# The expert stage of an attention and mixture-of-experts kernel: its engines put in one written order, weight splits placed between the products and their halves

## The chip, the cores and the metric

One core of one Trainium2 chip runs the kernel as a single launch. The metric is the device time of one execution in microseconds (us). The engines are TensorE (PE in the profile, with its weight loads apart as PEld), VectorE (DVE), ScalarE (ACT), GpSimd (POOL) and SyncE (SP, whose queue issues most of the transfers).

## What is computed

Three stages follow each other: causal attention with a bias, a mixture of 8 experts of which each token uses one, and a dense two-layer network on the experts' outputs.

```python
attn = softmax(q @ k.T / 8 + min(bias, 0), causal) @ v      # 4 x 8 heads, 576 tokens, 64 wide
x = attn as 2304 rows of 512
e = argmax(x @ w_gate); gate = softmax(x @ w_gate)[e]
x = gate * (relu(x @ w1[e]) @ w2[e])                        # w1 512 x 1024, w2 1024 x 512, per expert
h = x @ w_in; out = (h * clip(h + 3, 0, 6) / 6) @ w_out     # 512 x 2048, 2048 x 512
```

All of it is wanted in float32 quality. The kernel splits each float32 number into a 16-bit high half and a 16-bit rest, and each product of two matrices becomes three matmuls (high by high, high by rest, rest by high).

## The kernel before

The change is in the expert stage. It runs 10 **passes** over sorted tokens: two of 224 rows for experts 0 and 1 (passes 0 and 1), then one for each expert, the fullest first, of 336, 336, 336, 312, 296, 280, 136 and 104 rows (passes 2 to 9). A pass has an **f half**, eight first products `ph` (`expert_hidden`, L1002, 12 matmuls each), and a **d half**, four second products `py` (L1090, 24 matmuls each).

- After a first product ACT writes the high half of `hT` (`Relu`, L1006) and DVE the rest (L1007). A second product reads all eight of them, `hT` 0 first. After a second product DVE multiplies by the tokens' gates (`y`, L1096, from the transfer `held`, L1056), ACT writes the high half into `x2T` (L1097) and POOL the rest (L1098). ACT also fills the part of `x2T` that a pass may leave over with zeros (L1069, four times in a pass).
- The weights of pass p + 1 are loaded and split during pass p. They are eight **pieces** of 512 KB (`wf`, L228, on SP's queue), four of `w1` and four of `w2`, into five buffers. In passes 2 to 7 two further pieces hold the dense network's `w_in` (`wd`, L967), which arrives as **doubles**: ACT takes the absolute value (L972), POOL bounds it (L974), DVE shifts and joins (L975, L979, L980), ACT writes the high half (L981), DVE the rest (L982).
- `piece(..., act)` says who splits. False: POOL writes the high half (L239), DVE the rest (L240). True: ACT writes the high half (L237). 2: ACT writes the high half (L232), POOL scales in place (L233) and writes the rest (L234), and DVE has no part.
- The tokens of pass p + 1 come by a chain of transfers: `slots` (the list of rows, L200, SP), a gather `xg` of 128 rows at a time (L207, POOL), and a transpose of each gathered tile into `xsT` (L211, SP).
- `feed(k)`, called after each product, issues up to k loads and lets the oldest of them be split while more than four are outstanding. A split is one call: all the instructions of the piece.

In the attention stage the order on each engine is fixed by `in_order`. In the expert stage it is not: a scheduler arranges the instructions of each engine by its own estimate, held only by dependencies and by a few `issue_after` marks. Each engine then runs its list strictly from the front, so an instruction that waits holds up all behind it.

Pass 0 also takes in the last attention units' router work: three small products (`pl`, L608), `route`, `place_tokens` (which writes each token's row to `tok_d` by five scatters, L677) and `counts`, by the list `hooks`. `slots` of pass 2 and later can only be read behind those scatters.

Of the kernel before, what the change touches and what calls it, by code (L numbers as in the profile page):

```python
# [33 lines left out]
def kernel(  # L34
# [225 lines left out]
    def w2_jobs(src, ring="even", act=False):  # L260
# [6 lines left out]
                lambda f: f.rearrange("p (a n) -> p a n", a=2), act,  # L267
# [4 lines left out]
    with ExitStack() as at:  # L272
# [584 lines left out]
        for us in groups:  # L857
# [9 lines left out]
            for g, u in sorted(enumerate(us), key=lambda x: place[x[1]]):  # L867
# [7 lines left out]
                if us[0] == min(late) and place[u] >= NU - 3:  # L875
                    hooks.setdefault(min(len(hooks), 4), []).append(lambda u=u, mms=mms: mms[u]())
                    continue
                at_time(t + d, lambda u=u, mms=mms: mms[u]())
                routed = max(routed, t + d + 1.0)
            if us[0] == min(late):  # L880
                hooks.setdefault(4, []).append(lambda us=us: list(route(us)))
                hooks.setdefault(4, []).append(lambda us=us: (list(place_tokens(us)), counts()))
# [15 lines left out]
        w0 = w1_jobs(of(0), act=2)  # L898
        splits = {}

        def w_load(x):
            if x == len(w0):
                w0.extend(w2_jobs(of(0), act=2))
# [56 lines left out]
    def double_piece(src, hi, lo):  # L960
# [4 lines left out]
        def ld():  # L965
# [3 lines left out]
            def sp():  # L969
# [4 lines left out]
                gts(out=mf, in0=mf, scalar1=3.0e38, scalar2=2.0**-15, op0=ALU.min, op1=ALU.max)  # L974
                nc.vector.tensor_scalar(  # L975
# [20 lines left out]
    def expert_hidden(wt, xT, n, hT, f):  # L996
# [3 lines left out]
        for c in range(KD):  # L1000
            for x, (a, b_) in enumerate(((0, 0), (0, 1), (1, 0))):
# [3 lines left out]
                ).ins  # L1005
        mark["act"] = nc.scalar.activation(hT[0][:, f, :n], ph[:, :n], AF.Relu).ins  # L1006
# [13 lines left out]
    with ExitStack() as ex_:  # L1020
# [5 lines left out]
        xsT = xs0[0]  # L1026
        for p, rows in enumerate(passes):
            jobs = []
            nxt = None
            if p + 1 < NPASS:  # L1030
                nxt = load_x(p + 1)
                ring = "even" if p % 2 else "odd"
                jobs = w1_jobs(of(p + 1), ring, p == 0) + w2_jobs(of(p + 1), ring, p == 0)
                if 2 <= p <= 7:
                    jobs += djobs[:2]
                    del djobs[:2]
            hT = [e2.tile([128, KF, CAP], F16, tag=f"hT{x}", name="hT") for x in range(2)]
            wt1, wt2 = wts[p % 2], wts[2, p % 2]
            pend, fed = [], [0]

            def feed(k):
                for ld in jobs[:k]:
                    with tc.issue_after(mark["x" if fed[0] < KD or ("xs", 1) not in mark else ("xs", 1)]):
                        pend.append(ld())
                    fed[0] += 1
                del jobs[:k]
                while len(pend) > (8 if hooks else 4 if jobs else 0):
                    with tc.issue_after(mark["pos"]):
                        pend.pop(0)()

            for f in range(KF):
                expert_hidden(wt1, xsT, rows, hT, f)
                if f == 4:
# [7 lines left out]
                if p == 0:  # L1061
                    for h in hooks.pop(f, []):
                        h()
                if p and f % 2 == 1:

                    a, z = (min(sum(passes[:x]), NT) for x in (p, p + 1))
                    if z > a:
                        with after("act"):
                            nc.scalar.activation(  # L1069
                                x2T[:, f // 2::KD, a:z], zero16[:, None].to_broadcast([128, 2, z - a]), AF.Copy  # L1070
                            )
                feed(1 + f % 2)
            if NS <= p + 2 < NPASS:
                load_slots(p + 2)
# [10 lines left out]
            for d in range(KD):  # L1085
# [8 lines left out]
                hi, lo = x2T[:, d, at_], x2T[:, KD + d, at_]  # L1094
# [5 lines left out]
            xsT = nxt  # L1100
# [181 lines left out]
```

## Time and profile before

| | |
|---|---|
| median of 3 runs | 968.99 us (967.59 to 971.37) |
| the profiled execution's own time | 966.54 us |
| its span, first to last instruction | 964.8 us |
| mean granted TensorE clock | 0.932 of full speed |
| busy in the span: PE, DVE, ACT, POOL | 87%, 56%, 36%, 43% |
| expert stage, first `ph` to the first product of the dense network | 264.1 to 561.7 us |

Times in views are from the span's start. The span is 1.7 us shorter than the execution. Busy time of PE counts matmuls at whatever clock was granted, so a slow clock looks like work.

### The profile page before, as it was taken

Reading aid. Unit: us, or ns where it says so; the run is one execution under the profiler, and the core shown is the slowest. Engines: PE = TensorE matmul, PEld = TensorE weight load, DVE = VectorE, ACT = ScalarE, POOL = GpSimd, SP = SyncE. Lnnn points to the kernel's source line nnn. Section 1 sums busy time; section 2 is a strip of 40 time slices with the busy share of each in tenths; the row PEclk is TensorE's granted clock in tenths of the full one; section 3 lists DMA queues with packets and bytes.
Section 4 is the critical chain, followed back from the end, with each engine's and each line's share of the span. In section 5 each row is a group of like instructions: output and inputs, shape, how many; then the busy total and the mean of one; then the engine's idle time right before and its main releaser. Section 6 shows DMA issues by size and latency. Waiting matters only on the chain. (4 is left out here: it accounts for less than half of the span.)

```text
span 964.8 us, 17003 instructions
## 1 busy us (share of the span) xinstructions
PE 843.3 (87%) x6402; PEld 516.6 (54%) x6402; DVE 545.1 (56%) x1206; ACT 345.7 (36%) x684; POOL 410.6 (43%) x451
## 2 busy tenths in 40 slices
PE   7899998888785968888887799987999999999993
PEld 5566666655574735556665654433444444447441
DVE  5668877768544658967677649997044025105000
ACT  5687677665532303223222234433022012002000
POOL 2863564954735747745734624442022012112010
PEclk9899999779787979889989899997999999999997
DMA  9788649324577997797879513321000000000000
GB/s 244 164 163 214 112 100 266 67 78 89 96 183 171 205 230 236 212 263 178 265 158 204 160 43 108 124 88 45 34 12 0 22 22 1 12 22 12 22 23 24
DMA packets 140746, 112.71 MB, mean 117 GB/s; under 512 B 114760, under 2 KB 115024, under 8 KB 140144
## 3 DMA queue, kind: packets, MB, share of 16 engines
q1 hardware_dynamic: 136816, 101.43, 44.5%
q0 software_dynamic: 3840, 10.12, 3.2%
q8 instruction: 52, 0.85, 0.4%
q14 instruction: 38, 0.31, 0.1%
HBM read 91.82 MB, written 9.62 MB: 105 GB/s over the span
## 5 line engine op out<-in xcount | busy, mean ns | idle before, releaser
L1014 PE MATMUL py<-wo,gT 128*128 128x512 f16 x864 | 190.8, 383 | 5.7 <-ACT wo L981 3.8
L1109 PE MATMUL ph<-x2T,wi 128*128 128x512 f16 (+1 forms) x960 | 188.2, 358 | 4.0 <-DVE t L1115 3.5
L1090 PE MATMUL py<-hT,t 128*128 128x336 f16 (+6 forms) x960 | 121.1, 288 | 29.4 <-DVE hT L1007 20.8
L1109 PEld LDWEIGHTS <-wi 128*128 128x128 f16 x960 | 93.9, 98 | 97.6 <-issue 5.5
L240 DVE SCALAR_TENSOR_TENSOR t<-wf,t 128x1024 f16<-128x1024 f32 x72 | 109.8, 1536 | 63.8 <-POOL t L239 51.0
L1014 PEld LDWEIGHTS <-gT 128*128 128x128 f16 x864 | 85.2, 99 | 110.4 <-issue 10.8
L1002 PE MATMUL ph<-xsT,t 128*128 128x336 f16 (+6 forms) x960 | 117.8, 286 | 27.1 <-DVE nblk L737 11.4
L1115 DVE SCALAR_TENSOR_TENSOR t<-t,ph 128x512 f32<-128x512 f32 (+1 forms) x80 | 50.3, 630 | 137.7 <-ACT t L1114 137.7
L1090 PEld LDWEIGHTS <-t 128*128 128x128 f16 x960 | 88.9, 102 | 60.7 <-issue 34.0
L1002 PEld LDWEIGHTS <-t 128*128 128x128 f16 x960 | 89.9, 103 | 52.6 <-issue 27.9
L239 POOL TENSOR_SCALAR t<-wf 128x1024 f16<-128x1024 f32 x64 | 83.2, 1304 | 53.3 <-DMA wf<-in_moe_w_dram 52.5
L1116 POOL TENSOR_SCALAR gT<-t 128x512 f16<-128x512 f32 (+1 forms) x80 | 53.9, 674 | 120.0 <-DVE t L1115 119.6
L513 DVE SCALAR_TENSOR_TENSOR P<-pt,P 128x512 f16<-128x512 f32 (+3 forms) x128 | 73.0, 572 | 49.3 <-ACT P L507 47.5
L501 PE MATMUL pt<-idf,ne 128*128 128x128 f32 (+1 forms) x400 | 76.9, 305 | 18.1 <-ACT ne L493 15.2
L493 ACT ACTIVATE ne<-ne,nm 128x256 f32<-128x256 f32 (+4 forms) x144 | 80.2, 579 | 26.7 <-DVE nm L487 26.1
L1150 POOL DMA_INDIRECT out_dram<-o,orows x18 | 17.9, 995 | 165.1 <-ACT o L1148 155.7
L1114 ACT ACTIVATE t<-ph,three 128x512 f32<-128x512 f32 (+1 forms) x80 | 50.9, 641 | 89.6 <-PE ph L1109 86.9
L458 PE MATMUL sp<-kT,qT 64*128 64x256 f32 (+3 forms) x256 | 69.6, 539 | 6.9 <-DVE nm L487 6.9
L1117 DVE SCALAR_TENSOR_TENSOR gT<-t,gT 128x512 f16<-128x512 f32 (+1 forms) x80 | 57.2, 716 | 32.2 <-POOL gT L1116 32.2
L1148 ACT ACTIVATE o<-py 128x512 f32<-128x512 f32 x18 | 10.7, 597 | 165.3 <-PE py L1014 165.3
L507 ACT ACTIVATE P<-pt 128x512 f16<-128x512 f32 (+3 forms) x128 | 63.3, 494 | 18.3 <-PE pt L501 18.0
L501 PEld LDWEIGHTS pt<-idf,ne 128*128 128x128 f32 (+1 forms) x400 | 47.2, 149 | 41.5 <-ACT ne L493 31.6
(163 smaller groups left out, 999.0 us busy)
## 6 DMA issues: line engine op xcount, KB each, us to landing
wf<-in_moe_w_dram SPq DMA_DIRECT2D x80, 512.0 KB, 7.1
cp<-cum_d SPq DMA_DIRECT2D x4, 2304.0 KB, 10.9
wd<-in_moe_w_in_dram SPq DMA_DIRECT2D x16, 512.0 KB, 8.6
wd<-in_moe_w_out_dram SPq DMA_DIRECT2D x16, 512.0 KB, 3.5
k<-in_k_dram SPq DMA_DIRECT2D x16, 256.0 KB, 4.2
q<-in_q_dram SPq DMA_DIRECT2D x16, 256.0 KB, 4.9
v<-in_v_dram SPq DMA_DIRECT2D x16, 256.0 KB, 5.2
x_d<-xw SPq DMA_DIRECT2D x16, 256.0 KB, 2.3
```

Source lines behind the costliest of these rows:

```text
L239: gts(out=hi, in0=fv, scalar1=sc, scalar2=1.0, op0=ALU.mult, op1=ALU.mult)
L240: stt(out=lo, in0=fv, scalar=sc, in1=hi, op0=ALU.mult, op1=ALU.subtract)
L458: nc.tensor.matmul(self.sp[e][:, :W], qT[h, p, q0:q0 + 128], kT[h, p, :W], start=True, stop=not self.early)
L493: mark["act"] = nc.scalar.activation(self.view(e), self.view(e), AF.Exp, bias=self.nm[:, e:e + 1], scale=-1.0).ins
L501: nc.tensor.transpose(self.pt[g][:m, x, :], self.view(e)[:, 128 * j:128 * j + m], idf)
L507: nc.scalar.activation(self.half[g][0], self.half[g][2], AF.Copy, scale=SP)
L513: stt(out=lo, in0=pt, scalar=SP, in1=hi, op0=ALU.mult, op1=ALU.subtract)
L1002: mark["pe"] = nc.tensor.matmul(ph[:, :n], wt[:, a, c, cols], xT[:, KD * b_ + c, :n], start=(c == 0 and x == 0), stop=(c == KD - 1 and x = ...
L1014: nc.tensor.matmul(py[:n], hT[i_][:, f, a:a + n], wt[:, j_, f, :], start=(f == 0 and x == 0), stop=(f == nk - 1 and x == 2),)
L1090: nc.tensor.matmul(py[:, :rows], wt2[:, j_, f, cols], hT[i_][:, f, :rows], start=(f == 0 and x == 0), stop=(f == KF - 1 and x == 2),)
L1109: nc.tensor.matmul(ph[:, :n], wi[:, a, kk, fs], x2[:, KD * b_ + kk, :n], start=(kk == 0 and x == 0), stop=(kk == KD - 1 and x == 2),)
L1117: stt(out=gT[1][:, f, :n], in0=t, scalar=SG, in1=gT[0][:, f, :n], op0=ALU.mult, op1=ALU.subtract)
```

## The change

- `in_order` is now called for the whole expert stage: PE, ACT, DVE, POOL and SP run in the order in which the program writes them.
- `split()` is the new visit to the oldest loaded piece. It is called inside `expert_hidden` behind the matmuls of product f and ahead of the two halves of `hT` f (f = 1, 3, 5, 7; in passes 2 to 7 f = 1, 2, 3, 5, 6, 7), and behind each second product.
- `fill()` keeps five pieces loaded or loading. The jobs are one list over all passes (`more`): the `w1` pieces of pass p + 2 join it behind the f half of pass p, its `w2` pieces and two doubles behind the d half.
- A double is converted in two visits: ACT's and POOL's first two steps, and at the next visit the rest (`finish`).
- Who splits is `mixed = (True, 2, True, True)`: ACT takes the high half of every piece; of four pieces DVE writes the rest of three and POOL of one.
- The gather of pass p + 1 stands behind f = 1 (f = 4 in pass 1) and its transposes behind f = 6, both in pass p; `slots` of pass p + 2 is read at the end of pass p; `held` is loaded at f = 0, ahead of the products.
- ACT's and POOL's halves of a `y` are written one second product later (`put`).
- In pass 0 the router products stand behind f = 4, 5 and 6, and the steps of `route` and `place_tokens` behind the f half (two) and behind the second products (four each).

```diff
-    def w1_jobs(src, ring="even", act=False):
+    def w1_jobs(src, ring="even", act=(False,) * 4):
...
-            piece(src(w1, 128 * c, 128), t[:, 0, c], t[:, 1, c], S1, lambda f: f, act)
+            piece(src(w1, 128 * c, 128), t[:, 0, c], t[:, 1, c], S1, lambda f: f, act[c])
...
                 gts(out=mf, in0=mf, scalar1=3.0e38, scalar2=2.0**-15, op0=ALU.min, op1=ALU.max)
+                return lambda: finish(m, mf, low, high)
+
+            def finish(m, mf, low, high):
                 nc.vector.tensor_scalar(
...
+        if between:
+            between()
         mark["act"] = nc.scalar.activation(hT[0][:, f, :n], ph[:, :n], AF.Relu).ins
...
+        first = len(nc.cur_bb.bb.instructions)
+        mixed = (True, 2, True, True)
+        jobs, pend, nxt = [], [], {}
+        def more(p, second):
+            if p < NPASS:
+                ring = "even" if p % 2 == 0 else "odd"
+                jobs.extend((w2_jobs if second else w1_jobs)(of(p), ring, mixed))
+            if second and 3 <= p <= 8:
+                jobs.extend(djobs[:2])
+                del djobs[:2]
+        def fill():
+            while jobs and len(pend) + len(rest) < 5:
+                pend.append(jobs.pop(0)())
+        rest = []
+        def split():
+            if pend:
+                then = pend.pop(0)()
+                if rest:
+                    rest.pop()()
+                    fill()
+                if then:
+                    rest.append(then)
+                else:
+                    fill()
+            elif rest:
+                rest.pop()()
+        def put():
+            if ready:
+                hi, lo, y = ready.pop()
+                nc.scalar.activation(hi, y, AF.Copy)
+                gtt(out=lo, in0=y, in1=hi, op=ALU.subtract)
...
         for p, rows in enumerate(passes):
-                nxt = load_x(p + 1)
-                jobs = w1_jobs(of(p + 1), ring, p == 0) + w2_jobs(of(p + 1), ring, p == 0)
...
-            def feed(k):
-                for ld in jobs[:k]:
-                    with tc.issue_after(mark["x" if fed[0] < KD or ("xs", 1) not in mark else ("xs", 1)]):
-                        pend.append(ld())
...
             for f in range(KF):
-                expert_hidden(wt1, xsT, rows, hT, f)
-                if f == 4:
+                if f == 0:
...
+                expert_hidden(wt1, xsT, rows, hT, f, split if f in ((1, 2, 3, 5, 6, 7) if extra else (1, 3, 5, 7)) else None)
+                if f == (4 if p == 1 else 1) and p + 1 < NPASS:
+                    nxt["x"] = gather(p + 1)
+                if f == 6 and p + 1 < NPASS:
+                    nxt["t"] = turn(p + 1, nxt["x"])
...
+                if p == 0 and f >= 4 and hooks.get("mm"):
+                    hooks["mm"].pop(0)()
+            if p == 0:
+                for _ in range(2):
+                    next(hooks["steps"], None)
+            more(p + 2, False)
+            fill()
...
-                nc.scalar.activation(hi, y, AF.Copy)
-                gtt(out=lo, in0=y, in1=hi, op=ALU.subtract)
-                feed(2)
+                put()
+                ready.append((x2T[:, d, at_], x2T[:, KD + d, at_], y))
+                if p == 0:
+                    for _ in range(4 if d < 3 else 0):
+                        next(hooks["steps"], None)
+                    if d == KD - 1:
+                        counts()
+            put()
+            if p + 2 < NPASS and p + 2 >= NS:
+                load_slots(p + 2)
+            more(p + 2, True)
+            fill()
+        in_order(first, (mybir.EngineType.PE, mybir.EngineType.Activation, mybir.EngineType.DVE, mybir.EngineType.Pool, mybir.EngineType.SP))
```

What this does to the engines' lists shows in pass 3. These are DVE's rows in its f half before (`t` are the split weights, `hT` the rests of the eight first products):

```order
L1007 SCALAR_TENSOR_TENSOR hT<-ph,hT 128x336
L240 SCALAR_TENSOR_TENSOR t_5981<-wf,t_5981 128x1024 x2
L1007 SCALAR_TENSOR_TENSOR hT<-ph,hT 128x336 x3
L240 SCALAR_TENSOR_TENSOR t_5981<-wf,t_5981 128x1024
L1007 SCALAR_TENSOR_TENSOR hT<-ph,hT 128x336
L240 SCALAR_TENSOR_TENSOR t_5992<-wf,t_5992 128x1024 x2
L1007 SCALAR_TENSOR_TENSOR hT<-ph,hT 128x336
L240 SCALAR_TENSOR_TENSOR t_5992<-wf,t_5992 128x1024
L1007 SCALAR_TENSOR_TENSOR hT<-ph,hT 128x336
L240 SCALAR_TENSOR_TENSOR t_5992<-wf,t_5992 128x1024
L1007 SCALAR_TENSOR_TENSOR hT<-ph,hT 128x336
```

And now, where `m` is the second half of the double that pass 2 began:

```order
L1011 SCALAR_TENSOR_TENSOR hT<-ph,hT 128x336
L240 SCALAR_TENSOR_TENSOR t_5829<-wf,t_5829 128x1024
L977 TENSOR_SCALAR m<-m 128x512
L981 SCALAR_TENSOR_TENSOR m<-wd,m 128x512
L982 SCALAR_TENSOR_TENSOR m<-wd,m 128x512
L984 SCALAR_TENSOR_TENSOR wi<-m,wi 128x512
L1011 SCALAR_TENSOR_TENSOR hT<-ph,hT 128x336 x2
L240 SCALAR_TENSOR_TENSOR t_5829<-wf,t_5829 128x1024
L1011 SCALAR_TENSOR_TENSOR hT<-ph,hT 128x336 x2
L240 SCALAR_TENSOR_TENSOR t_5829<-wf,t_5829 128x1024
L1011 SCALAR_TENSOR_TENSOR hT<-ph,hT 128x336
L240 SCALAR_TENSOR_TENSOR t_5991<-wf,t_5991 128x1024
```

Before, seven splits stood among the eight `hT`, four of them between the last four. Now it is four splits and one half of a double (two `hT` follow the piece shown).

ACT's rows in the same f half before hold no split at all (L1006 is `hT`'s high half, L1069 the zeros, L972 the first step of a double):

```order
L1006 ACTIVATE hT<-ph 128x336 x2
L1069 ACTIVATE x2T<-zero_78 128x2x336
L1006 ACTIVATE hT<-ph 128x336 x2
L1069 ACTIVATE x2T<-zero_78 128x2x336
L1006 ACTIVATE hT<-ph 128x336 x2
L1069 ACTIVATE x2T<-zero_78 128x2x336
L1006 ACTIVATE hT<-ph 128x336 x2
L972 ACTIVATE m<-wd 128x512
L1069 ACTIVATE x2T<-zero_78 128x2x336
L972 ACTIVATE m<-wd 128x512
```

Now ACT has six splits (L237, L232) and the high half of a double (L983) among the same eight `hT`:

```order
L1010 ACTIVATE hT<-ph 128x336
L237 ACTIVATE t_5829<-wf 128x1024
L983 ACTIVATE wi<-m 128x512
L1010 ACTIVATE hT<-ph 128x336
L1115 ACTIVATE x2T<-zero_78 128x2x336
L232 ACTIVATE t_5829<-wf 128x1024
L1010 ACTIVATE hT<-ph 128x336
L237 ACTIVATE t_5829<-wf 128x1024
L1010 ACTIVATE hT<-ph 128x336
L1115 ACTIVATE x2T<-zero_78 128x2x336
L1010 ACTIVATE hT<-ph 128x336
L237 ACTIVATE t_5829<-wf 128x1024
```

The first five `hT` are shown; each of the last three has a split right ahead of it.

SP's queue in pass 3 before issues the transposes for pass 4 with doubles' loads between them, and `slots` for pass 5 right ahead of them:

```order
L228 DMA wf<-in_moe_w_dram 128x2x512
L200 ISA
L200 DMA slots<-tok_d 128x3x3
L211 DMA_TRANSPOSE xsT<-xg 128x8x128
L967 DMA wd<-in_moe_w_in_dram 128x1024
L211 DMA_TRANSPOSE xsT<-xg 128x8x128
L967 DMA wd<-in_moe_w_in_dram 128x1024
L211 DMA_TRANSPOSE xsT<-xg 128x8x80
```

Now the doubles' loads come first and the three transposes for pass 4 stand together:

```order
L228 DMA wf<-in_moe_w_dram 128x2x512
L966 DMA wd<-in_moe_w_in_dram 128x1024 x2
L1087 DMA_TRANSPOSE xsT<-xg 128x8x128 x2
L1087 DMA_TRANSPOSE xsT<-xg 128x8x80
L164 TENSOR_LOAD dyn_i
L164 ISA x2
L228 ISA
L228 DMA wf<-in_moe_w_dram 128x1024
```

`slots` for pass 5 moved from ahead of the transposes to the pass's end, behind the load shown last and three more like it. In the program, the gather that reads it follows after f = 1 of the next pass.

## Rows read from the trace of the kernel before

**Rows 1.** The page's 40 equal slices: the clock granted to TensorE, in tenths
```profile
PEclk9899999779787979889989899997999999999997
```

**Rows 2.** Stretches: us, busy per engine (count), granted clock, DMA share, GB/s
```profile
264.00:323.40 59.40, 43.45 (x430) 40.63 (x431) 29.74 (x85) 17.96 (x37) 28.23 (x23) 0.85 0.82 187
323.40:531.30 207.90, 170.86 (x1155) 117.16 (x1153) 150.58 (x171) 57.38 (x118) 121.32 (x105) 0.92 0.88 216
531.30:552.80 21.50, 14.58 (x195) 13.89 (x193) 14.40 (x22) 4.65 (x16) 14.86 (x15) 0.84 0.47 133
552.80:561.70 8.90, 8.76 (x192) 8.76 (x192) 2.33 (x9) 2.06 (x8) 0.00 (x0) 1.00 0.49 175
561.70:964.80 403.10, 378.02 (x1829) 179.12 (x1825) 156.56 (x245) 85.60 (x142) 89.76 (x122) 0.97 0.11 35
```

**Rows 3.** Timeline of PE in the expert stage: start, length, count, idle before
```profile
351.34 13.03 PE L1090 MATMUL py<-hT,t 128*128 128x336 f16 x73 [3.34 <-DVE hT L1007]
...
402.81 13.84 PE L1002 MATMUL ph<-xsT,t 128*128 128x336 f16 x96
...
501.28 10.17 PE L1002 MATMUL ph<-xsT,t 128*128 128x280 f16 x84
...
544.84 5.84 PE L1090 MATMUL py<-hT,t 128*128 128x136 f16 x96 [0.51 <-DVE hT L1007]
...
557.34 4.56 PE L1090 MATMUL py<-hT,t 128*128 128x104 f16 x96
```

**Rows 4.** Waits from 262 to 562 us: total, times, longest
```profile
POOL t L239 <- DMA wf<-in_moe_w_dram: 52.5, 30, 7.6
DVE t L240 <- POOL t L239: 51.0, 32, 3.8
...
PE py L1090 <- DVE hT L1007: 20.8, 13, 4.2
```

**Rows 5.** Groups by shape, 262 to 562 us: busy us, mean ns, idle before
```profile
L979 DVE SCALAR_TENSOR_TENSOR m<-wd,m 128x512 int32<-128x512 int32 x12 | 10.7, 892 | 0.2
...
L1006 ACT ACTIVATE hT<-ph 128x336 f16<-128x336 f32 x24 | 10.2, 445 | 10.1 <-PE ph L1002 10.1
...
L1069 ACT ACTIVATE x2T<-zero 128x672 f16<-128x672 f16 x12 | 9.1, 759 | 0.0
...
L237 ACT ACTIVATE t<-wf 128x1024 f16<-128x1024 f32 x8 | 8.4, 1054 | 25.1 <-DMA wf<-in_moe_w_dram 25.1
...
L981 ACT ACTIVATE wi<-m 128x512 f16<-128x512 f32 x12 | 7.6, 630 | 32.9 <-DVE m L980 32.9
```

**Rows 6.** Three lines of the splits: duration ns min/median/max, first and last start
```profile
L233 POOL TENSOR_SCALAR wf<-wf x8: 1039/1044/1087, 152.6 to 259.2; 128x1024 f32<-128x1024 f32 x8
...
L234 POOL TENSOR_TENSOR t<-wf,t x8: 2124/2126/2136, 153.7 to 260.3; 128x1024 f16<-128x1024 f32 x8
...
L240 DVE SCALAR_TENSOR_TENSOR t<-wf,t x72: 1204/1226/3849, 288.1 to 546.9; 128x1024 f16<-128x1024 f32 x72
```

**Rows 7.** Landing of slots, gathers xg and transposes xsT, 262 to 562 us
```profile
DMA to landing us min/median/max: 4.2/8.4/14.7
...
DMA to landing us min/median/max: 4.2/7.7/13.6
...
DMA to landing us min/median/max: 4.4/6.6/12.1
```

**Rows 8.** Stretches of 1 us around the transposes of pass 4 (columns of rows 2)
```profile
417.00:418.00 1.00, 1.00 (x9) 0.69 (x8) 0.00 (x0) 0.00 (x0) 0.71 (x1) 1.00 1.03 408
...
424.00:425.00 1.00, 0.07 (x1) 0.00 (x0) 1.00 (x3) 0.43 (x1) 0.00 (x0) 0.50 1.15 43
```

**Rows 9.** Timeline: first and last scatter of pass 0, first slots behind them
```profile
282.67 1.02 POOL L677 DMA_INDIRECT tok_d<-what,pos_s  x1 [14.24 <-DVE acc L687]
...
287.85 0.93 POOL L677 DMA_INDIRECT tok_d<-what,pos_s  x1 [0.30 <-issue]
...
291.76 0.38 SPq L200 DMA_DIRECT2D slots<-tok_d  x1
```

More of the change, by code (lines that the diff above doesn't have):

```diff
@@ L880 @@
             if us[0] == min(late):
-                hooks.setdefault(4, []).append(lambda us=us: list(route(us)))
-                hooks.setdefault(4, []).append(lambda us=us: (list(place_tokens(us)), counts()))
+                hooks["steps"] = chain(route(us), place_tokens(us))
                 continue
@@ L897 @@
                 at_slot(n0 + 9, lambda: xs0.append(load_x(0)))
-        w0 = w1_jobs(of(0), act=2)
+        w0 = w1_jobs(of(0), act=(2,) * 4)
         splits = {}
@@ L994, with expert_hidden @@
     ]
-    def expert_hidden(wt, xT, n, hT, f):
+    def expert_hidden(wt, xT, n, hT, f, between=None):
         ph = pb.tile([128, 512], F32, tag="p", name="ph")
@@ new lines, with gather @@
+        ready = []
+        def put():
[3 more added lines that the diff above has]
+                gtt(out=lo, in0=y, in1=hi, op=ALU.subtract)
+        def gather(p):
+            n = passes[p]
+            got = []
+            for x, (a, m) in enumerate(blocks((n + 15) // 16 * 16)):
+                xg = row_tile([128, 2 * DM], F16, "xg")
+                nc.gpsimd.indirect_dma_start(
+                    out=xg[:m], out_offset=None, in_=x_d[:min(col0[u] for u in late) if p < NS else NT, :],
+                    in_offset=Offset(ap=slots[:m, p, x, 0:1], axis=0),
+                )
+                got.append((a, m, xg))
+            return got
@@ L1037, with turn @@
+        def turn(p, got):
+            t = (rings["odd"] if p % 2 else rt).tile([128, 2 * KD, (CAP + 15) // 16 * 16], F16, tag="xsT", name="xsT", bufs=1)
+            for a, m, xg in got:
+                nc.sync.dma_start_transpose(out=t[:, :, a:a + m], in_=xg[:m])
+            return t
+        more(1, False)
+        more(1, True)
+        fill()
+        for p, rows in enumerate(passes):
+            extra = 2 <= p <= 7
             hT = [e2.tile([128, KF, CAP], F16, tag=f"hT{x}", name="hT") for x in range(2)]
@@ L1038 @@
             wt1, wt2 = wts[p % 2], wts[2, p % 2]
-            pend, fed = [], [0]
-            def feed(k):
-                for ld in jobs[:k]:
-                    with tc.issue_after(mark["x" if fed[0] < KD or ("xs", 1) not in mark else ("xs", 1)]):
-                        pend.append(ld())
[L1045 to L1049, printed above, removed]
@@ L1067 @@
                     if z > a:
[L1068 to L1074, printed above, removed]
+                        nc.scalar.activation(
+                            x2T[:, f // 2::KD, a:z], zero16[:, None].to_broadcast([128, 2, z - a]), AF.Copy
+                        )
+                if p == 0 and f >= 4 and hooks.get("mm"):
[5 more added lines that the diff above has]
+            fill()
             if p == 1:
@@ L1093 @@
                         )
-                hi, lo = x2T[:, d, at_], x2T[:, KD + d, at_]
+                split()
                 y = row_tile([128, CAP], F32, "y")[:, :rows]
                 nc.vector.tensor_tensor(out=y, in0=py[:, :rows], in1=g, op=ALU.mult)
-                nc.scalar.activation(hi, y, AF.Copy)
-                gtt(out=lo, in0=y, in1=hi, op=ALU.subtract)
-                feed(2)
-            xsT = nxt
+                put()
[9 more added lines that the diff above has]
+            more(p + 2, True)
+            fill()
+            xsT = nxt.get("t")
+        while jobs or pend or rest:
+            fill()
+            split()
+        in_order(first, (mybir.EngineType.PE, mybir.EngineType.Activation, mybir.EngineType.DVE, mybir.EngineType.Pool, mybir.EngineType.SP))
     def hidden(pool, gT, x2, f, n):
@@ L1139, in hidden_of @@
                 while len(pend) > (2 if jobs else 0):
-                    pend.pop(0)()
+                    pend.pop(0)()()
             return gT
```

18 lines of the change are left out of this document (4 added, 14 removed).

## The prediction

> **What bounds the kernel now.** I read the clock by slices first, then the stretches, then PE's timeline with what ended its idle time, then the waits. The slices show a clock of 10 tenths through most of the last stage and dips to 7 and 8 in the middle [rows 1]. The stretches put numbers on it: passes 0 and 1 take 59.4 us, passes 2 to 7 207.9 us, pass 8 21.5 us, pass 9 8.9 us, and what follows 403.1 us [rows 2]. In passes 2 to 7 PE is busy for 170.9 us at a mean clock of 0.92, so it idles 37 us and loses more to the lower clock [rows 2].
>
> What would these passes take without a wait? An unbroken f half of 336 rows takes 13.84 us, and 84 matmuls of 280 rows take 10.17 us, so 11.6 us for 96 [rows 3]. Two halves each: 27.7 us and 23.2 us; 312 and 296 rows lie on the line between, 25.8 and 24.5. Passes 2 to 7 come to 3 x 27.7 + 25.8 + 24.5 + 23.2 = 156.6 us, so 51 us of their 207.9 are lost. Pass 8 would take 2 x 5.84 = 11.7 us, and pass 9 is at its product time [rows 3].
>
> The waits say how they are lost. PE's second products wait 20.8 us in 13 pieces for DVE's `hT`; DVE waits 51.0 us, in 32 pieces, for POOL's high half of a weight piece; POOL waits 52.5 us for that piece's load [rows 4]. This is one chain: seven splits stand in DVE's list among the eight `hT`, and when a load is late the `hT` behind it is late too. After such a wait of 3.34 us, 73 matmuls of 336 rows took 13.03 us instead of 73 x 0.144 = 10.5 [rows 3]: the clock costs another 2.5 us.
>
> The last stage, 403.1 us, keeps its instructions and their durations; I leave it as it is.
>
> **The change, part by part.**
>
> *Splits between products and five loads ahead.* In a pass with doubles a piece is loaded five visits before it is split, and ten visits share 27.7 us, so a load has some 13 us. It landed in a median of 7 to 8 us like the transfers of [rows 7]. So I let the chain of late loads vanish. What must still be in time is `hT` 6 and 7, read by the first second product after 18 of its 24 matmuls, 13.84 + 18 x 0.144 = 16.4 us into the pass.
>
> *ACT takes the high halves.* Its f half now holds six splits of 1.054 us, eight `hT` of 0.445, four zero fills of 0.759 and a double's high half of 0.630 [rows 5]: 6.3 + 3.6 + 3.0 + 0.6 = 13.5 us, in a half of 13.84. And at f = 1 ACT must wait for DVE: a split (1.2 us, [rows 6]) and three steps of a double (0.6 to 0.9 us each by L979's 0.892, [rows 5]) come first, some 3 us. From the first `ph` at 1.7 us the last `hT` then leaves ACT at about 17.9 us and DVE at 18.4. PE waits about 2 us at the first second product of each pass that finishes a double (3 to 7). ACT's list hardly shrinks with the rows, the products do: I take 2.0, 2.0, 2.5, 3.0 and 3.3 us, 12.8 us. The bounds are nothing, if ACT's wait is shorter, and 13.5 + 3 + 1.7 - 13.84 = 4.4 us in each of the five, 22 us.
>
> *POOL's part.* It gives up 48 of its 64 high halves and takes 18 scalings (1.044 us) and 18 rests (2.126 us, [rows 6]), two of each in a pass, 6.3 us. By these rows that is hidden beside 27 us of products. It also takes part of DVE's time, since DVE's rest took 1.226 us in the median but up to 3.849 [rows 6]; DVE's waits in the d half cost PE nothing while the five product buffers last, so I add nothing.
>
> *The chain that brings the next pass's tokens.* `slots` is issued at the end of a pass, lands in 8.4 us (4.2 to 14.7), three gathers are issued at 1.3 us each and land in 7.7 (4.2 to 13.6), three transposes follow and each lands in 6.6 (4.4 to 12.1) [rows 7]. With `slots` at 5 us into the pass, since the queue ahead of it is then short, the gathers are there at 13 to 14 us, and three transposes at 4.4 to 5 us each end at 27 to 28 us: just before the 28 to 30 us that a pass then lasts. I take 1 us for each of six passes, 6 us, for it being late or for the clock after it; the bounds are nothing and the 12.1, 13.6 and 14.7 of the rows, which is the slow rival below. In pass 8, which has 11.7 us of products, one gather and one transpose cannot be hidden: 5 + 1 + 6 + 5.5 = 17.5 us. I take 18 us for it, 9 us for pass 9.
>
> The Trainium skill, "Advanced Engine Details and Errata", X-Bar Transpose (TRN2), says that transposing transfers are as fast as plain ones. The row does not agree: in the midst of the transposes of pass 4 the core moved 43 GB/s, just before them 408 [rows 8]. By the page's 350 to 400 GB/s the three transposes, 0.7 MB, would take 2 us, an estimate; the chain would then never be late in passes 2 to 6 and 4 us shorter in pass 8, and the sum below would be 921 us.
>
> *Passes 0 and 1.* The router's products move behind f = 4 to 6, where the last transposed unit is there (PE waited for it before), and the rank products from inside the f half to behind the first second product. The f half of pass 0 ends near 277 us, the first second product at 279.4, the ranks follow behind the second, at 284. POOL first has a split (3.2 us, [rows 6]) and a `put`, so the five scatters, which ran from 282.67 to 288.8, run from 287 to 293.6; `slots`, issued 3.0 us behind the last one before (291.76), is issued at 297 [rows 9]. From there the least of the rows, 4.2 + 4.2 + two or three transposes, gives pass 2's tokens at 315 us, the medians 326. PE has finished passes 0 and 1 by then (306 us by two times 2 x 9.7 and the waits). I take 321 us: 57 us instead of 59.4. Pass 2 then begins at the low clock, another 2.5 us.
>
> *The sum.* Passes 2 to 7: 156.6 + 12.8 + 6 + 2.5 = 178 us instead of 207.9. All: 2.4 + 29.9 + 3.5 (pass 8) = 36 us. 966.5 of the profiled execution less 36 is **931 us**; its time lies 2.4 us under the median of the runs, which is within what they scatter.
>
> **The rivals.**
>
> *Nothing but products.* If ACT's wait and the chain of tokens hide, passes 2 to 7 take 158 us, pass 2 starts at 315 and pass 8 takes 15: 966.5 - 8 - 50 - 6.5 = 902, with a little clock 905 us. For it: no PE wait in the stage names ACT's own work now. Against it: 13.5 us of ACT in 13.84 leave no room. The Trainium skill's page on transposes, named above, is on this side, and its row is not.
>
> *The transfers bound it.* Passes 2 to 7 moved 216 GB/s at a share of 0.88 [rows 2], 45 MB. In 178 us that is 252 GB/s. The rows reach 408 in a full microsecond and 43 with transposes [rows 8], and six passes of three transposes at some 5 us hold a half of the time. If the mean stays at 230, the passes take 195 us: 948 us.
>
> *The fixed order turns into a new wait, and it is slower.* POOL stands at the gather until `slots` is there; behind it stands its part of the second piece, behind that the buffer, SP's next load and the transposes. With the slow ends of rows 7, 14.7 + 3.9 + 13.6 and three transposes ending 12 to 20 us later, the tokens come 45 to 50 us into a pass. Halfway, at 42 us, five passes lose 12 us each: 990 us. It decides from about 37 us. Against it: these ends were reached in a queue with up to five loads ahead, at `slots` there is now one or two.
>
> *It does not do what it says.* Without the late loads another release, with the same 51 us, would come last in each pass: 966 us. DVE's seven splits among the `hT` are the named cause, so this is unlikely.
>
> **How the numbers follow.** The forecast has 0.50 (918 to 944, from half of ACT's term to the upper end of the tokens' term in passes 0 and 1), the products alone 0.17, the transfers 0.21, the slower one 0.07, no change 0.05. The range of 8 in 10 leaves out the lowest part of the products' case and the last two: 903 to 958 us. A change under 0.5%, 5 us, could not be told from none here. Faster: 0.50 + 0.17 + 0.21 and nothing of the rest, 0.88; the same 0.04; slower 0.08.
>
> **What would show it.** In the changed kernel's profile: the waits of the second products for DVE's `hT` fall from 20.8 us to 10 to 15, in pieces of 2 to 3 us, one at the start of the d half of passes 3 to 7, with ACT busy just before; DVE's waits for a weight piece fall below 20 us; pass 2 starts between 315 and 326 us with PE waiting for `xsT` before it; PE waits for `xsT` again before pass 9; passes 2 to 7 take 170 to 190 us at a clock above 0.95; what follows pass 9 takes 403 us. The forecast is wrong if PE waits for `xsT` by 5 us or more before each of passes 3 to 7, if ACT waits for loads, or if the last stage grows.

## The result and the profile after

The changed kernel takes **980.80 us** (median of 3 runs, 979.19 to 983.97) against 968.99: a ratio of 1.0135, with a 95% interval from 1.0094 to 1.0176. It is slower by 1.35%, and 50 us above the forecast of 931. Its profiled execution takes 979.19 us, with a span of 977.5.

First the stretches that answer to [rows 2], with the same columns: passes 0 and 1, passes 2 to 7, pass 8, pass 9, what follows.

```profile
270.80:328.90 58.10, 42.44 (x431) 39.60 (x432) 33.53 (x86) 26.13 (x46) 32.64 (x27) 0.88 0.83 207
328.90:537.40 208.50, 168.17 (x1153) 115.56 (x1154) 109.32 (x149) 101.36 (x164) 95.28 (x74) 0.95 0.80 201
537.40:560.10 22.70, 13.49 (x192) 12.87 (x193) 15.35 (x23) 12.14 (x23) 11.85 (x9) 0.92 0.96 201
560.10:574.20 14.10, 10.46 (x193) 10.35 (x193) 4.71 (x16) 3.10 (x13) 2.79 (x5) 0.86 0.71 63
574.20:977.50 403.30, 378.99 (x1824) 179.15 (x1823) 156.21 (x242) 85.29 (x141) 89.99 (x122) 0.97 0.11 37
```

Passes 2 to 7 were to take 178 us and take 208.5, as before (207.9). PE is busy for 168 us of them and the transfers run at 201 GB/s, less than before, so neither is full. Against the forecast the profiled execution is 48 us long: 6.7 because the expert stage starts at 270.8 instead of 264.1, 1 in passes 0 and 1, 30.5 in passes 2 to 7, 5 in pass 8, 5 in pass 9, nothing in the last stage.

PE's timeline (as [rows 3]) at the start of passes 2 to 8, with the wait for the pass's tokens where there is one (pass 3 has none):

```profile
328.89 14.91 PE L1004 MATMUL ph<-xsT,t 128*128 128x336 f16 x84 [10.16 <-DMA xsT<-xg]
364.71 12.13 PE L1004 MATMUL ph<-xsT,t 128*128 128x336 f16 x84
397.67 10.42 PE L1004 MATMUL ph<-xsT,t 128*128 128x336 f16 x72 [2.66 <-DMA xsT<-xg]
432.04 9.70 PE L1004 MATMUL ph<-xsT,t 128*128 128x312 f16 x72 [1.50 <-DMA xsT<-xg]
467.39 12.40 PE L1004 MATMUL ph<-xsT,t 128*128 128x296 f16 x84 [4.61 <-DMA xsT<-xg]
503.69 12.59 PE L1004 MATMUL ph<-xsT,t 128*128 128x280 f16 x84 [4.76 <-DMA xsT<-xg]
537.37 3.79 PE L1004 MATMUL ph<-xsT,t 128*128 128x136 f16 x60 [2.45 <-DMA xsT<-xg]
```

The starts lie 33 to 36 us apart, for 336 rows and for 280: a period that doesn't follow the products points to a loop of something else. The waits of the stage (columns of [rows 4]) name its members; `issue` is idle time for which the view names no release:

```profile
ACT t L237 <- DMA wf<-in_moe_w_dram: 49.2, 18, 7.5
POOL xg L1077 <- issue: 43.9, 17, 13.5
POOL xg L1077 <- DMA slots<-tok_d: 30.3, 3, 11.5
PE ph L1004 <- DMA xsT<-xg: 29.6, 7, 10.2
PE ph L1004 <- DVE hT L1011: 19.6, 10, 4.4
PE py L1140 <- DVE hT L1011: 9.9, 13, 1.6
```

SP's own queue, in the same stretch, waits longest for POOL's rests of weight pieces before it can issue a load:

```profile
SPq L228 <- POOL t L234: 49.2, 9, 8.8
```

POOL stands at the gathers, ACT waits for pieces that come late, PE's first products wait for `xsT` and for halves of `hT` held up behind those pieces, and SP's loads wait for POOL. Pass 5 (432.0 to 467.4 us) shows the loop whole. SP's queue and POOL there:

```profile
429.09 1.26 SPq L1087 DMA_TRANSPOSE xsT<-xg  x1
...
433.08 1.54 SPq L228 DMA_DIRECT2D wf<-in_moe_w_dram  x3
435.45 0.40 SPq L200 DMA_DIRECT2D slots<-tok_d  x1
436.46 0.63 SPq L1101 DMA_DIRECT2D held<-tok_d  x1
439.16 18.42 SPq L228 DMA_DIRECT2D wf<-in_moe_w_dram  x4
457.69 0.88 SPq L966 DMA_DIRECT2D wd<-in_moe_w_in_dram  x2
458.67 6.96 SPq L1087 DMA_TRANSPOSE xsT<-xg  x3
```

```profile
448.00 1.04 POOL L1077 DMA_INDIRECT xg<-x_d,slots  x1 [11.49 <-DMA slots<-tok_d]
449.34 1.66 POOL L1077 DMA_INDIRECT xg<-x_d,slots  x1 [0.30 <-issue]
451.30 1.50 POOL L1077 DMA_INDIRECT xg<-x_d,slots  x1 [0.30 <-issue]
452.88 1.05 POOL L233 TENSOR_SCALAR wf<-wf 128x1024 f32<-128x1024 f32 x1
454.01 3.18 POOL L234 TENSOR_TENSOR t<-wf,t 128x1024 f16<-128x1024 f32 x1
```

The list `slots` goes out at 435.45, behind the transposes and four loads. POOL idles 11.49 us for it, so it landed near 448, and issues its gathers until 452.8; only then comes its part of the weight piece, until 457.2. That piece holds a buffer (SP's wait for L234 above), and SP's four loads are drawn out over 18.42 us, until 457.6. The transposes stand behind them in SP's list, so they start at 458.67, and the next `slots` stands behind these. Where [rows 9] had the first scatter of pass 0 at 282.67 and `slots` at 291.76, both follow later than I forecast (287 and 297):

```profile
289.33 0.66 SPq L1134 DMA_DIRECT2D row_d<-tok_d  x1
...
310.89 0.38 SPq L200 DMA_DIRECT2D slots<-tok_d  x1
...
301.41 1.09 POOL L677 DMA_INDIRECT tok_d<-what,pos_s  x1 [7.56 <-DVE begin_i L731]
```

### The profile page after: what moved, and what is told of

Read it like the earlier page. It is cut to its first block, busy times and chain, and to the rows that moved or that the text cites. A ratio compares the mean times of both kernels' runs of the same rounds, so it can differ in the third digit from the quotient of the medians.

```text
span 977.5 us, 17016 instructions
## 1 busy us (share of the span) xinstructions
PE 845.1 (86%) x6402; PEld 515.1 (53%) x6402; DVE 509.2 (52%) x1188; ACT 406.0 (42%) x748; POOL 389.3 (40%) x423
## 5 line engine op out<-in xcount | busy, mean ns | idle before, releaser
L1004 PE MATMUL ph<-xsT,t 128*128 128x336 f16 (+6 forms) x960 | 123.7, 294 | 51.0 <-DMA xsT<-xg 29.6
L1004 PEld LDWEIGHTS <-t 128*128 128x128 f16 x960 | 91.8, 106 | 81.7 <-DMA xsT<-xg 27.9
L1140 PE MATMUL py<-hT,t 128*128 128x336 f16 (+6 forms) x960 | 110.8, 273 | 12.8 <-DVE hT L1011 9.9
L240 DVE SCALAR_TENSOR_TENSOR t<-wf,t 128x1024 f16<-128x1024 f32 x54 | 76.6, 1418 | 60.2 <-ACT t L237 58.5
L1140 PEld LDWEIGHTS <-t 128*128 128x128 f16 x960 | 84.9, 98 | 37.8 <-issue 17.0
L458 PE MATMUL sp<-kT,qT 64*128 64x256 f32 (+3 forms) x256 | 71.9, 559 | 11.3 <-DVE nm L487 8.8
L237 ACT ACTIVATE t<-wf 128x1024 f16<-128x1024 f32 x54 | 56.9, 1054 | 49.8 <-DMA wf<-in_moe_w_dram 49.2
```

The costliest lines, as they stand in the source:

```text
L237: nc.scalar.activation(hi, fv, AF.Copy, scale=sc)
L240: stt(out=lo, in0=fv, scalar=sc, in1=hi, op0=ALU.mult, op1=ALU.subtract)
L458: nc.tensor.matmul(self.sp[e][:, :W], qT[h, p, q0:q0 + 128], kT[h, p, :W], start=True, stop=not self.early)
L1004: mark["pe"] = nc.tensor.matmul(ph[:, :n], wt[:, a, c, cols], xT[:, KD * b_ + c, :n], start=(c == 0 and x == 0), stop=(c == KD - 1 and x = ...
L1140: nc.tensor.matmul(py[:, :rows], wt2[:, j_, f, cols], hT[i_][:, f, :rows], start=(f == 0 and x == 0), stop=(f == KF - 1 and x == 2),)
```

## The experiments

Each ratio is to runs of the kernel before on the same chip, whose medians were 963.4 to 966.5 us in these comparisons. Differences given in us are of medians; against the changed kernel, which was timed beside a median of 968.99, the ratios make gains over it about 5 us smaller (24 instead of 29 for slots_early) and the loss of no_fixed_order 2 us larger. "Passes 2 to 7" runs from the first product of pass 2 to that of pass 8, "stage" from the first product of pass 0 to the first of the dense network, both in one trace.

| version | median us | ratio to before (95%) | passes 2 to 7 | stage |
|---|---|---|---|---|
| before (as in [rows 2]) / before_again | 968.99 / 961.57 | | 207.9 / 201.7 | 298 / 287 |
| changed | 980.80 | 1.0135 (1.0094 to 1.0176) | 208.5 | 303 |
| slots_early | 951.68 | 0.9888 (0.9823 to 0.9954) | 181.5 | 275 |
| no_pool_split | 943.64 | 0.9801 (0.9726 to 0.9875) | 180.7 | 273 |
| gather_f3 | 961.42 | 0.9988 (0.9964 to 1.0012) | 189.8 | 283 |
| only_six | 953.03 | 0.9893 (0.9857 to 0.9929) | 182.9 | 277 |
| slots_early_no_pool | 947.46 | 0.983 (0.977 to 0.989) | 182.7 | 273 |
| no_fixed_order | 990.41 | 1.026 (1.0196 to 1.0324) | 213.0 | 318 |
| short_chain_no_order | 974.64 | 1.0124 (1.0099 to 1.0149) | 209.5 | 305 |
| old_shares | 976.95 | 1.0155 (1.0132 to 1.0179) | 200.1 | 300 |
| rows_first | 943.71 | 0.9777 (0.9739 to 0.9814) | 182.7 | 265 |
| loads_later | 946.64 | 0.9797 (0.9757 to 0.9837) | 182.7 | 273 |
| rows_and_loads | 941.45 | 0.977 (0.972 to 0.982) | 184.2 | 268 |
| six_buffers | 927.99 | 0.9629 (0.9603 to 0.9656) | 173.3 | 258 |
| six_with_pool | 937.81 | 0.9736 (0.9699 to 0.9773) | 173.6 | 257 |

**slots_early.** The list is read a pass earlier, at f = 0 behind `held`.

```diff
+                    if p and p + 2 < NPASS:
+                        load_slots(p + 2)
...
-            if p + 2 < NPASS and p + 2 >= NS:
-                load_slots(p + 2)
+            if p == 0:
+                load_slots(2)
```

> The changed kernel with one transfer moved: the list of tokens of pass p + 2 is read at the start of pass p instead of at its end (pass 2's own list stays where it is). Theory 1, the fixed order hangs on that list: GpSimd no longer waits 11 us for it at the gather, the transposes end before the products do, passes 2 to 7 fall from 208 us to 170 to 185 us, and the whole from 981 to 945 to 957 us. Theory 2, the transfers bound the passes at some 200 GB/s: passes 2 to 7 stay at 200 to 208 us and the whole within 973 to 981 us. Theory 3, what is late are the weight pieces that ScalarE must split among its halves of hT: the wait for the tokens goes but waits of the products for hT take half of its place, passes 2 to 7 take 190 to 198 us, the whole 963 to 971 us.

951.68 us, 29 below the changed kernel, and 181.5 us for passes 2 to 7: theory 1. Pass 5 of this kernel, POOL and SP:

```profile
426.25 1.04 POOL L1077 DMA_INDIRECT xg<-x_d,slots  x1
...
428.43 9.78 SPq L228 DMA_DIRECT2D wf<-in_moe_w_dram  x4
...
441.67 6.75 SPq L1087 DMA_TRANSPOSE xsT<-xg  x3
```

The gather waits for nothing, the four loads go out in 9.78 us instead of 18.42, and the transposes start 18 us after the pass (423.56) instead of 27. SP's wait for POOL's rests falls from 49.2 to 10.9 us. Of 29.6 us of waits for `xsT` 13.9 are left, 13.5 of them before pass 2.

**no_pool_split.** The list stays late; DVE writes the rest of every piece.

```diff
-        mixed = (True, 2, True, True)
+        mixed = (True, True, True, True)
```

> The changed kernel with VectorE writing the rest of all four pieces, so that GpSimd has no weight work behind its gather. If what costs time is the second piece that stands behind the waiting gather, and with it the buffer and SyncE's next load, passes 2 to 7 fall by 15 to 30 us and the whole to 950 to 965 us. If the chain from the list of tokens to the gathers and the transposes alone is too long (list at 16 us into a pass, gathers to 19, landed at 27, transposes to 34), the passes keep 33 to 36 us each and the whole stays within 975 to 983 us. If VectorE's further split of 1.3 us in each half is on the path, it is up to 8 us slower.

943.64 us, passes 2 to 7 in 180.7: the chain of the tokens by itself is not too long. POOL still idles some 10 us or more ahead of the gathers of passes 3 to 7, but no weight piece is behind them, and SP waits for no POOL rest.

**slots_early_no_pool** has both edits.

> Both edits: the early list of tokens and no weight work on GpSimd. If the list of tokens is the whole cause, it equals the early list alone within 4 us. If GpSimd's piece behind the gather still holds a buffer when the list is early, it is 5 to 12 us faster than the early list alone; if VectorE then has too much among its halves of hT, 3 to 8 us slower.

947.46 us lies within 4.3 us of either, and the intervals overlap (4.2 us to slots_early, just beyond the 4 us expected for one cause): both edits open the same loop, and it can be opened only once.

**gather_f3.** List and shares as in the changed kernel, but the gather stands behind the first weight piece.

```diff
-                if f == (4 if p == 1 else 1) and p + 1 < NPASS:
+                if f == (4 if p == 1 else 1 if p == 0 else 3) and p + 1 < NPASS:
```

> The changed kernel with the gather of passes 3 to 9 written behind f = 3 instead of f = 1, so that GpSimd's first weight piece of a pass stands ahead of the gather that waits for the late list, and everything else as in the changed kernel, GpSimd's share too. Theory: what costs time is that piece behind the waiting gather (its buffer, SyncE's next load, the transposes behind that load); then passes 2 to 7 fall from 208 to 178 to 190 us and the whole from 981 to 945 to 963 us, although the gather is written later. Rival: it is GpSimd's use of VectorE's time, or ScalarE's wait for GpSimd, that the version without GpSimd's weight work removed; then the passes stay at 200 us or above and the whole at 973 us or above.

961.42 us, 19 below the changed kernel, by writing an instruction *later*. In pass 5 POOL's piece is done at 439.9, and the gather at 440.06 waits 0.15 us. SP's wait for POOL's rests is 5.1 us instead of 49.2. POOL's share and ACT's wait for it are thus not the main cause. It gains less than the early list; what is left are waits for `hT`, of the second products 21.3 us against 13.2 in slots_early, of the first 17.7 against 7.6.

**only_six.** The changed kernel with one buffer more.

```diff
-        stage.update({0: ex_.enter_context(tc.tile_pool(name="ste", bufs=5)), 1: "wf"})
+        stage.update({0: ex_.enter_context(tc.tile_pool(name="ste", bufs=6)), 1: "wf"})
...
-            while jobs and len(pend) + len(rest) < 5:
+            while jobs and len(pend) + len(rest) < 6:
```

> The changed kernel with six weight buffers and six loads ahead, and nothing else: the list of tokens is as late as in the changed kernel and GpSimd's piece stands behind the gather. If the loop closes through the buffer that this piece holds (SyncE's next load and the transposes behind it wait for that buffer), one buffer more opens it: passes 2 to 7 fall from 208 to 175 to 190 us and the whole from 981 to 945 to 965 us. If GpSimd's wait for the list is by itself the limit, or only both together with the edits in pass 0 help, the passes stay at 198 us or above and the whole at 970 us or above.

953.03 us. POOL still waits for the list, 52.8 us in 6 pieces, and its piece still stands behind the gather. SP's loads and transposes in pass 5 of this kernel:

```profile
429.92 7.22 SPq L228 DMA_DIRECT2D wf<-in_moe_w_dram  x3
444.93 0.83 SPq L966 DMA_DIRECT2D wd<-in_moe_w_in_dram  x2
445.87 6.10 SPq L1087 DMA_TRANSPOSE xsT<-xg  x3
```

The last of `wf` is out at 437, before POOL begins its piece at 441.64. Only the doubles' loads wait for the piece: it ends at 444.90, they go out at 444.93, and the transposes follow 21 us into the pass. In the changed kernel the piece ends at 457.19 and the same loads go out at 457.69, with the transposes 27 us in. So the loop closes through the buffer. Not all of the gain need be the loop's: a sixth buffer is worth 13 us in six_buffers below, where the loop is open already.

**no_fixed_order** and **short_chain_no_order.** The changed kernel, and slots_early_no_pool, without the fixed order.

```diff
         while jobs or pend or rest:
             fill()
             split()
-        in_order(first, (mybir.EngineType.PE, mybir.EngineType.Activation, mybir.EngineType.DVE, mybir.EngineType.Pool, mybir.EngineType.SP))
```

> The changed kernel without the fixed order of the expert stage: the scheduler arranges each engine's instructions again, and splits, loads and gathers stay as written otherwise. If the fixed order is what makes the new wait, passes 2 to 7 fall to 180 to 198 us and the whole to 953 to 970 us. If it is the later list of tokens whatever the order, or the share that ScalarE took, the passes stay at 205 us or above and the whole at 977 us or above.

> The version with the early list of tokens and no weight work on GpSimd, without the fixed order: what the order itself is worth once the new wait is gone. The changed kernel without the order took 990 us, 10 more than with it. If the order is worth by itself what the kernel before lost to splits among the halves of hT, this takes 970 us or more, 23 above the same version in order. If the order is worth little and the early list and the shares do it, it stays within 945 to 955 us.

990.41 and 974.64 us. My guess that the order as such made the wait is wrong: without it each is slower, by 10 us and by 27. PE's waits in short_chain_no_order:

```profile
PE ph L1004 <- DVE y L1148: 26.6, 9, 5.2
PE ph L1004 <- DMA xsT<-xg: 19.9, 3, 16.6
```

The first row is new: first products wait for a product buffer, which `y` sets free. From 290 us on DVE, which writes `y`, waits 76.5 us in 23 pieces for ACT's halves of weight pieces there, 30.4 us in the same version in order, where PE's wait for `y` is not among its waits of 2 us or more. The order is worth 27 us where its own chain is short, and the changed kernel could show only 10 of it.

**old_shares.** The early list, with POOL and DVE splitting as in the kernel before.

```diff
-        mixed = (True, 2, True, True)
+        mixed = (False, False, False, False)
```

> The changed kernel with the early list of tokens and the shares of the kernel before: GpSimd writes the high half of every piece and VectorE the rest, ScalarE none. If ScalarE's six splits in the f half were what the products still wait for (13.2 us for hT in the version with the early list), this is 3 to 10 us faster than it, 941 to 949 us. If GpSimd's pieces stand behind its gathers and slow VectorE as they did before (waits of VectorE for them of 51 us), it is 5 to 20 us slower, 957 to 972 us.

976.95 us, 25 more than slots_early and 5 above the slower branch, so ACT's share is a gain. DVE waits for POOL's half again, as in [rows 4], and PE's first products for `hT`:

```profile
DVE t L240 <- POOL t L239: 52.0, 30, 12.1
...
PE ph L1004 <- DVE hT L1011: 26.5, 8, 8.5
```

**rows_first, loads_later, rows_and_loads** start from slots_early_no_pool and change pass 0: the small read into `row_d` goes to f = 0, behind `held` (the first two pieces of the diff), or the first five loads go behind the last transposes of the attention stage (the last piece), or both.

```diff
+                    if p == 0:
+                        nc.sync.dma_start(row_d[:rows], rows_of(0, rows)[:, 2:3])
...
-            nc.sync.dma_start(row_d[at_], rows_of(p, rows)[:, 2:3])
+            if p:
+                nc.sync.dma_start(row_d[at_], rows_of(p, rows)[:, 2:3])
...
-        fill()
+        with tc.issue_after(mark["x"]):
+            fill()
```

> The version with the early list of tokens and no weight work on GpSimd, and in pass 0 the small read of tok_d into row_d issued at f = 0 instead of behind the f half. Theory: the five scatters into tok_d have their positions at 293 us but start at 300 us, since that read of tok_d stands ahead of them and lands late behind weight loads; without it they start at 293 to 295 us, the list of pass 2 is issued at 306 instead of 311 us, the products' wait for pass 2's tokens falls from 13.4 to 6 to 8 us, and the whole from 947 to 940 to 943 us. Rival: the scatters wait for another release, GpSimd's or VectorE's order; then they start at 300 us again and the time stays within 945 to 950 us.

> The version with the early list of tokens and no weight work on GpSimd, and the first five weight loads of the expert stage held behind the last two transposes of the attention stage, as the kernel before holds them. Theory: these 2.6 MB ahead of the last transposes make the last router product wait 3 us and pass 2's list late by as much; then the wait for pass 2's tokens falls from 13.4 to 10 us, and the whole to 942 to 946 us. Rival: the loads that come 3 us later are missed by pass 1's splits; then passes 0 and 1 are longer by 3 to 6 us and nothing is won, 946 to 952 us.

> Both edits in pass 0 together. If each takes its own part of the wait before pass 2, the wait falls to 3 to 5 us and the whole to 936 to 941 us; if they only relieve the same transfers, it equals the better one alone.

With the read moved, the scatters start 24.5 us after the first product of pass 0 (31.0 without the edit, 30.6 in the changed kernel), and the wait for pass 2's tokens falls from 13.4 to 3.2 us; passes 0 and 1 take 51.5 us instead of 58.1. The scatters had therefore waited for that read of `tok_d`, issued at 289.33 in the changed kernel in a queue full of weights; the views named something else, a DVE instruction in the changed kernel and a weight load in slots_early_no_pool. The median falls by 3.8 us only (943.71, just above the 940 to 943 of the theory), with overlapping intervals. Later loads cut the wait to 8.1 us but pass 1 starts later: passes 0 and 1 take 58.1 us again, 946.64, the rival. Both edits give 941.45; what they add to rows_first can't be told from nothing.

**six_buffers** adds the sixth buffer to rows_and_loads (diff as in only_six), **six_with_pool** puts POOL's share back into that.

> The version with both edits in pass 0 (941.5 us) with six weight buffers and six loads ahead instead of five. ScalarE still waits some 33 us in the stage for pieces that come late. If late pieces are what keeps passes 2 to 7 at 27 to 32 us against 23 to 28 us of products, it is 5 to 12 us faster, 930 to 937 us. If the transfers' rate bounds it, the sixth load only queues longer and it stays within 938 to 945 us.

> The fastest version so far (928 us: early list, both edits in pass 0, six buffers) with GpSimd's share of the changed kernel back, so one piece in four of GpSimd's rest. If that share is harmless once GpSimd doesn't wait at the gather, 925 to 932 us. If it slows VectorE or holds a buffer for longer, 934 to 945 us.

six_buffers takes 927.99 us, 3.7% less than the kernel before, the best of all and 2 us under the range expected. Its passes 2 to 7 beside those of rows_and_loads (columns of [rows 2]):

```profile
326.10:499.40 173.30, 162.05 (x1152) 114.94 (x1153) 115.69 (x164) 99.95 (x166) 45.14 (x53) 0.96 0.99 250
```

```profile
320.60:504.80 184.20, 165.12 (x1152) 115.58 (x1153) 115.16 (x162) 101.03 (x165) 43.70 (x52) 0.95 0.95 231
```

Nearly the same bytes (43 MB) move at 250 instead of 231 GB/s, so late pieces, not a ceiling of the transfers at 231, set the 182 us of the versions with five buffers. With POOL's share the median is 937.81, and the intervals of the two ratios don't overlap: by the timed runs the share costs some 10 us, the second branch. The traces don't show those 10 us, 173.6 us for passes 2 to 7 and the same stage, but they are of the slowest execution of six_buffers (934.06) and of the fastest of six_with_pool (929.48). What they do show is DVE's rest of a piece, 1.68 us in the mean with POOL's share and 1.22 without (300 to 500 us).

**before_again** is the kernel before, unchanged.

> The kernel before, unchanged, for a second trace. In the changed kernel and its four variants the first product of the expert stage starts at 269.0 to 271.7 us, in the one trace of the kernel before at 264.1 us. If the changed program makes the attention stage longer, it starts at 263 to 266 us here; if executions scatter, at 267 us or later.

The first product of its expert stage, in PE's timeline:

```profile
270.59 1.67 PE L1002 MATMUL ph<-xsT,t 128*128 128x224 f16 x8 [0.93 <-DVE xr L556]
```

It starts at 270.6 us. So the 6.7 us of the attention stage are scatter between executions and not the change's, and the trace shown before had a short attention stage and a long expert stage.

## Why the prediction was wrong

- **The failed step: "With `slots` at 5 us into the pass, since the queue ahead of it is then short, the gathers are there at 13 to 14 us".** That sum needs the list landed by 5 us (5, three issues of 1.3, a landing of 4.2). In pass 5 `slots` was only issued at 3.4 us and landed 16 us into the pass, the gathers were out at 21 us and the transposes began at 27. The queue ahead of it was not short: the transposes and four weight loads had just been issued. I had counted loads outstanding at a visit, not what stands between the transposes and the list in SP's written order. slots_early undoes this alone and gives 29 us back (24 by the ratios).
- **Passes 2 to 7 in the terms of the sum.** Products 156.6 us; PE's waits for tokens, from pass 3 to the start of pass 8, 16.0 us where I had 6; waits of first products for `hT` 14.7 us where I had nothing; waits of second products 9.4 us where I had 12.8; and PE is busy for 11.6 us more than the products, where I had 2.5 for a low clock (granted 0.95). That makes 208.3 of the 208.5 us. So the loop showed as late `hT` as much as late tokens, and my sign for it, 5 us or more of `xsT` before each of passes 3 to 7, did not come (0 to 4.8 us). Pass 2 takes 33 to 36 us with the loop open too (35.8 in slots_early, 34.8 in six_buffers): what the loop lengthens are passes 3 to 7.
- **What made it a loop.** POOL's piece behind the gather holds a buffer, the buffer SP's loads, these the transposes, and these the next list. Four edits each cut or widen one link (slots_early, no_pool_split, gather_f3, only_six), and each lowers the ratio to before by 0.015 to 0.033, 14 to 32 us. I had this mechanism as the slower rival, at 990 us and a chance of 0.07. I dismissed it by the short queue of the failed step, and I put the point from which it decides at 37 us. The loop's 33 to 36 us are already what a pass took before (207.9 / 6 = 34.7), so the whole gain was gone at that. The rival's own sum, 45 to 50 us, had slow landings, but neither the piece nor the loads that stand between the gathers and the transposes.
- **What made it slower than before, not only equal.** The expert stage takes 303 us, against 298 and 287 in the two traces of before. Those two differ by 11 us themselves, so that the kernel is slower rests on the timed runs. Passes 2 to 7 are 1 and 7 us longer than theirs, and passes 8 and 9, 36.8 us, are 6 and 9 us longer (30.4 and 28.0). The first part goes with the loop; of the second no run shows the cause: every version in order with ACT's shares waits 3 to 5 us for `hT` in the f half of pass 8 (1.8 and 2.3 before), and most wait 2 to 6 us for the last `x2T`.
- **"So I let the chain of late loads vanish".** It did not, as my own sign for a wrong forecast said ("if ACT waits for loads"): ACT waited 49.2 us for pieces (22.0 more for those that it shares with POOL), and PE 19.6 us in f halves for `hT` behind them. In slots_early ACT's wait falls to 26.9 us (14.4 more) and PE's to 7.6; six buffers bring passes 2 to 7 to 173.3 us, where I had 178, and there ACT still waits 17.0 us, in 3 pieces. So late loads shrink in a queue that runs freely, but they don't vanish.
- **ACT's last `hT`, 12.8 us, range 0 to 22.** PE's second products wait 9.9 us for `hT` in the changed kernel, 13.2 in slots_early. The size held; no run shows that ACT's full list is what makes these waits. old_shares shows that the shares are worth 25 us.
- **The order as a gain.** I took its effect through DVE's list; short_chain_no_order puts 27 us on the order itself.
- **Passes 0 and 1: 57 us forecast, 58.1 measured,** by errors that cancel. The scatters came 31 us after the first product instead of the 23 I worked out, since I overlooked that the read into `row_d` now precedes them; from the list to the tokens it then took 18 us instead of 24.
- **Slips in the working.** POOL gives up all 64 of its high halves, not 48 (`mixed` leaves it none); the sum doesn't use this. PE's waits before did name ACT's own work, 8.4 us of second products for its `hT`. Five scatters of 6.1 us from 287 end at 293.1, not 293.6. The ends named for the chance of 0.50 give 925 (half of ACT's term) and 936 (pass 2's tokens at 326 instead of 321), not 918 and 944.
- **Transposes.** By the 350 to 400 GB/s that the Trainium skill gives, "Advanced Engine Details and Errata", X-Bar Transpose (TRN2), the three transposes of a pass would take 2 us, an estimate. The trace doesn't agree: in pass 5 their issue alone spans 6.96 us of SP's queue, and 8.7 us pass from the first issue (458.67) to the product that waits for them (467.39). The comparison in [rows 8] is less clean than I took it for: the 408 GB/s did not lie ahead of the transposes, since the first of those three was issued at 415.0 and the other two at 422.2. Nor does pass 5 give the transposes' own rate: loads issued just ahead land in the same 8.7 us, in which the core moves 243 GB/s, 2.1 MB, and the transposes are 0.6 MB of it:

```profile
458.67:467.39 8.72, 4.11 (x32) 2.84 (x30) 3.36 (x6) 3.22 (x5) 4.47 (x4) 1.00 0.90 243
```

## What to carry to other kernels

When an order is fixed by hand, follow each small transfer through the queue that issues it: what is written ahead of it, what its consumer blocks while it waits, and whether that reaches back to the same queue; if it does, the period of the loop can be the bound, whatever the busy shares say. A period that doesn't change with the size of the work is a sign of it. A change that is slower can hold most of a gain: here the order was worth 27 us and the shares 25, each with the other in place, hidden by one list read too late and one buffer too few.

## What the runs showed that I had not expected

The start of the expert stage, after identical lists of instructions, lay at 264.1 and 270.6 us in two executions of the same kernel: 6.5 us of scatter in one stage, while whole executions of the kernel before lay between 957 and 971 us. A small read of 224 rows issued among weight loads held back scatters for 6 to 7 us, which the wait's named releaser didn't show. A sixth buffer raised the mean rate of the transfers in passes 2 to 7 from 231 to 250 GB/s.
